# Linear attention feeding two expert layers: reciprocal denominators of query blocks 0 and 1 spread by TensorE, key tiles in units of 1024 columns

## Chip, cores, metric

The kernel runs on one core of a Trainium2 chip. The metric is the device time of one execution in microseconds (us). Engines are called as the profile calls them: PE (TensorE matmul), PEld (its weight load), DVE (VectorE), ACT (ScalarE), POOL (GpSimd), SP (SyncE, which issues the DMAs).

## What is computed

Attention with a feature map instead of a softmax, then a gated feed-forward, then a soft mixture of experts on the 2304 tokens. The change touches the attention alone:

```
def phi(x):
    proj = np.einsum('bhsd,df->bhsf', x, w_phi)
    proj = proj - np.max(np.abs(proj), axis=-1, keepdims=True)
    return np.concatenate([np.exp(proj), np.exp(-proj)], axis=-1)
q_p, k_p = (phi(q), phi(k))
kv = np.einsum('bhsf,bhsd->bhfd', k_p, v)
z = np.sum(k_p, axis=2)
num = np.einsum('bhsf,bhfd->bhsd', q_p, kv)
den = np.einsum('bhsf,bhf->bhs', q_p, z)[..., None] + 1e-06
return (num / den).astype(np.float32)
...
x = rms_norm(attention) ; silu(x @ w_gate) * (x @ w_val) @ w_out ; soft mixture of experts
```

There are 4 batches of 576 tokens, 8 heads of 64, and 128 features (256 with both signs).

## The kernel before, in words

**Key stage.** The 2304 tokens are 18 tiles of 128 keys. For each tile, `project` (L387) multiplies the keys of all 8 heads by `w_phi`, into two PSUM tiles of one bank each (`P`, half 0 the even heads and half 1 the odd ones, 4 x 128 columns each). DVE takes the largest absolute value of each head's row (`mx`, L398) and subtracts it (`pr`, L402), a pass for each half. ACT writes exp(pr) and exp(-pr) (`kp`, L415 and L416), again by halves: four calls of 512 columns. PE then adds the tile into `kacc`: `kv_of` (L439) values times features, four matmuls for each half, and `z_of` (L448) the sums of features with a column of ones, 32 output columns wide, four side by side. The loop at L519 issues the projection of tile i+1 ahead of the sums of tile i. A tile that crosses a batch border is summed in two parts, so there are 20 sums. At a border the sums are copied out (`Evac`, `kvs`) and turned (`kvt`).

**Weights.** The feed-forward's weights come as 64-bit numbers. Nine of 18 pieces are converted within the key stage, nine within the first block of the feed-forward: DMA into `wraw`, two ACT passes (L127, L129), two DVE passes (L137, L139), a cast on ACT and a subtraction on POOL (L102, L105).

**Queries.** They come in six blocks of 384 tokens. Blocks 0 and 1 are `Turned`: their projections, transposes (`T`) and exponentials (`e`, L339) are put between the key tiles (block 0) and into the feed-forward's block 0 (query block 1) by tables of slots, `TURNED0` and `TURNED1`; a slot is half a key tile or a third of a feed-forward step. Blocks 2 to 5 are `Reduced`. All use `attend` (L197): for each pair of heads PE computes `num` (numerators, 128 x 384) and `den` (denominators, in rows of 32 equal partitions: heads by halves of the block, 192 columns). ACT copies `num` to SBUF, DVE adds 1e-6 and takes the reciprocal (L218, L219). Eight ACT copies of 32 x 192 (L224) spread the reciprocals to 64 partitions for each head, and DVE multiplies (L225). A square and a sum for the RMS norm follow (L228 to L232), then in other slots `scale` and `out`.

**Feed-forward.** Six blocks of 384 tokens, each of 12 steps of gate (`pg`), value (`pv`) and output (`acc`) matmuls. Gate block 0 needs query block 0 complete; its own fillers make query block 1. The experts follow.

What decides the order on each engine: the Tile framework orders the instructions within what the program's issue order and data allow. Each engine runs its queue in order.

Of the kernel before, what the change touches and what calls it, by code (L numbers as in the profile page):

```python
# [64 lines left out]
def tile_kernel(ctx: ExitStack, tc: tile.TileContext, q2T, qT, kT, v, wbd, wg, wv, wo, rmsg, phi, w1, w2, consts, out):  # L65
# [120 lines left out]
    class Q:  # L186
# [10 lines left out]
        def attend(self, c):  # L197
# [22 lines left out]
            rd = e[1][:, 0].rearrange("p (g t) -> p g t", g=2)  # L220
            for hh, g in halves:
                o = 64 * hh + 32 * g
                for r in range(2):
                    ACT.copy(out=rd[64 * hh + 32 * r:64 * hh + 32 * r + 32, g], in_=dn[o:o + 32])  # L224
            DVE.tensor_tensor(out=y, in0=y, in1=e[1][:, 0], op=ALU.mult)  # L225
# [7 lines left out]
            for b, t0, t1 in block_parts(self.blk):  # L233
                if c == 3 and self.blk * BLK + t1 == (b + 1) * SEQ and b + 2 < NB:
                    kvt[b + 2] = kvp.tile([128, NH, 2, HD + 1], F32, tag="kv", name=f"kv{b + 2}", bufs=2)
                    SP.dma_start(out=kvt[b + 2].rearrange("p h s d -> p (h s d)"), in_=kv_d[b + 2])

# [18 lines left out]
    class Reduced(Q):  # L256
# [43 lines left out]
        def steps(self):  # L300
            def first():
                self.split(0)
                self.load(3)

            f = [lambda h=h: self.feature(h) for h in range(NH)]
            a = [lambda c=c: self.attend(c) for c in range(4)]
            g = [lambda h=h: self.exps(h) for h in range(NH)]
            s = [first, *(x for c in range(4) for x in (f[2 * c], f[2 * c + 1], g[2 * c], g[2 * c + 1], a[c])), self.scale, self.out]
            return sorted(zip(REDUCED, s), key=lambda x: x[0])

    class Turned(Q):
# [28 lines left out]

        def spare(self):
            e = self.sp.tile([128, 2, 2, BLK], F32, tag="e", name="dg", bufs=self.bufs["e"])
            return e[:, 0, 0], None
# [10 lines left out]
        def steps(self, at, attend, end, lag=2):  # L354


            r, pr = [], {}

            def p(c, i):
                pr[c, i] = self.project(c, i)  # L360

            for c in range(4):
                for i in range(TPB):
                    r.append((at[c] + i, lambda c=c, i=i: p(c, i)))
                    r.append((at[c] + i + lag, lambda c=c, i=i: self.turn(c, i, pr[c, i])))
                r.append((attend[c], lambda c=c: self.attend(c)))
            r += [(end[0], self.scale), (end[1], self.out)]
            return sorted(r, key=lambda x: x[0])

    with ExitStack() as pk:  # L370
# [5 lines left out]
        class Front:  # L376


            def __init__(self, sp, ps, src, i, bufs):
                self.sp, self.ps, self.src, self.i, self.bufs, self.tag = sp, ps, src, i, bufs, bufs["tag"]  # L380
                self.mx, self.pr, self.e = {}, {}, {}
# [5 lines left out]
            def project(self):  # L387

                tag, n = self.bufs["P"]
                self.p = [self.ps.tile([128, 4, DF], F32, tag=tag, name="P", bufs=n) for _ in range(2)]  # L390
                for c in range(4):
                    for hf in range(2):
                        r = slice(64 * hf, 64 * hf + 64)
                        PE.matmul(out=self.p[hf][:, c], lhsT=self.raw[r, c], rhs=wbd_f[r, DF * hf:DF * hf + DF], start=True, stop=True)  # L394

            def largest(self, hf):
                self.mx[hf] = mx = self.sp.tile([128, 4, 1], F32, tag=self.tag + "mx", name="mx", bufs=2)
                DVE.tensor_reduce(out=mx, in_=self.p[hf], axis=AX.X, op=ALU.max, apply_absolute_value=True)  # L398

            def less(self, hf):  # L400
                self.pr[hf] = pr = self.sp.tile([128, 4, DF], F32, tag=self.tag + "pr", name="pr", bufs=self.bufs["pr"])
                DVE.tensor_tensor(out=pr, in0=self.p[hf], in1=self.mx[hf].to_broadcast([128, 4, DF]), op=ALU.subtract)  # L402

            def shift(self, hf):
                self.largest(hf)
                self.less(hf)

        class K(Front):
# [4 lines left out]
            def exps(self, hf):  # L413
                kp = sp.tile([128, 4, 2, DF], F32, tag="kp", name="kp", bufs=4)
                ACT.activation(out=kp[:, :, 0], in_=self.pr[hf], func=AF.Exp)  # L415
                ACT.activation(out=kp[:, :, 1], in_=self.pr[hf], func=AF.Exp, scale=-1.0)  # L416
                self.e[hf] = kp
# [11 lines left out]
            def kv_of(self, hf, part):  # L429
                kp = self.e[hf]  # L430
# [12 lines left out]
            def z_of(self, hf, part):  # L443
                kp, za = self.e[hf], acc[part[0]][2]
# [46 lines left out]
        kb = {"tag": "k", "raw": 4, "pr": 3, "P": ("P", 2)}  # L491
        SP.dma_start(out=wbd_f, in_=wbd)
        ks = [K(sp, psk, kT, i, kb if i else dict(kb, P=("misc", 3))) for i in range(TILES)]
# [17 lines left out]
        for hf in range(2):  # L511
            ks[0].shift(hf)
            ks[0].exps(hf)
# [5 lines left out]
        for i in range(TILES):  # L519
# [18 lines left out]
            if kn:  # L538
                kn.project()
                kn.shift(0)  # L540
                kn.largest(1)
                conv_join()
                kn.less(1)
            k.kv(parts[-1])
            for hf in range(2):
                if kn:
                    kn.exps(hf)
# [513 lines left out]
```

## Time and profile before

| what | us |
|---|---|
| three timed runs | 751.07, 747.67, 746.72 (median 747.67) |
| the profiled execution | 745.82 |
| its span, first to last instruction | 743.8 |
| PE busy in the span | 714.6 (96%) |
| DVE busy | 428.1 (58%) |
| ACT busy | 371.2 (50%) |
| POOL busy | 108.3 (15%) |

A busy time is the union of an engine's instructions. Matmul ends are modelled, so a busy PE need not be a PE at its peak: matmuls on different rows or columns of the array can run side by side, and whether they do is seen from the start of one group to the start of the next. Matmuls in fp32 have two records each, so `x16` is eight matmuls. The program's stages follow each other: keys until about 133 us, the feed-forward until about 687, then the experts, where DMA is the busiest.

### The profile page before, as it was taken

To read this page: it belongs to the slowest core of one execution; us is meant where nothing else is said; L and a number is where in the kernel's file an instruction comes from. 1 tells how busy PE (TensorE), PEld (TensorE's weight loads), DVE (VectorE), ACT (ScalarE), POOL (GpSimd) and SP (SyncE) were. 2 spreads that over 40 slices of the span, in tenths; PEclk is the share of its full clock that TensorE was granted. 3 is DMA by queue.
4 is the path that set the end of the run, shared out by engine and by line. 5 is a ranking of instruction groups with operands and counts; after the bars stand their busy time and mean duration, and the time that the engine had idled before them with its cause. 6 is when DMAs were issued, how large, how long until landed. Compare 5 with 4: busy or idle time off the path is not lost.

```text
span 743.8 us, 12360 instructions
## 1 busy us (share of the span) xinstructions
PE 714.6 (96%) x4919; PEld 576.0 (77%) x4919; DVE 428.1 (58%) x808; ACT 371.2 (50%) x805; POOL 108.3 (15%) x60
## 2 busy tenths in 40 slices
PE   6999898999899999999999999999999999999994
PEld 4555554888789888898888988889888899988343
DVE  5888956688746557555575565655556453332413
ACT  6789854688644465344653446533465331212102
POOL 0222210134200112011120121101211010000100
PEclk9999999999999999999999999999999999999997
DMA  9674211545010100101000010000100046567898
GB/s 321 231 251 171 72 44 45 200 158 200 1 61 22 33 22 22 48 0 33 22 23 20 1 33 22 23 19 0 33 1 2 9 170 248 204 227 291 292 385 312
DMA packets 25145, 79.45 MB, mean 107 GB/s; under 512 B 2688, under 2 KB 13376, under 8 KB 18688
## 3 DMA queue, kind: packets, MB, share of 16 engines
q1 hardware_dynamic: 24864, 77.79, 29.6%
q10 hardware_dynamic: 224, 0.88, 0.4%
q8 instruction: 38, 0.62, 0.4%
q14 instruction: 19, 0.16, 0.1%
HBM read 71.99 MB, written 6.67 MB: 106 GB/s over the span
## 4 chain that ended last, share of the span: by engine, by line
PE 73%; ACT 10%; DVE 6%; DMA 5%; issue 2%; POOL 1%; SPq 0%; ACTq 0%; DVEq 0%; POOLq 0%
PE pv L794 18%; PE pg L794 17%; PE acc L819 6%; PE acc L820 6%; PE acc L821 6%; PE num L206 4%; PE kacc L439 3%; DMA eu<-in_w_dram 2%; PE den L214 2%; ACT e L224 2%; PE kacc L448 2%; DVE wt L137 1%; DMA wraw<-in_wg_dram 1%; ACT wt L127 1%; PE P L394 1%
## 5 line engine op out<-in xcount | busy, mean ns | idle before, releaser
L794 PE MATMUL pv<-xnh,wv 128*128 128x384 f32 x576 | 151.5, 344 | 0.0
L794 PE MATMUL pg<-xnh,wg 128*128 128x384 f32 x576 | 150.2, 342 | 1.2 <-DVE t L802 1.0
L794 PEld LDWEIGHTS pg<-xnh,wg 128*128 128x128 f32 x576 | 104.7, 188 | 7.2 <-DVE t L802 1.5
L794 PEld LDWEIGHTS pv<-xnh,wv 128*128 128x128 f32 x576 | 103.1, 188 | 7.0 <-issue 6.7
L794 PE MATMUL pv<-xnl,wv 128*128 128x384 f32 x288 | 97.7, 339 | 0.0
L794 PE MATMUL pg<-xnl,wg 128*128 128x384 f32 x288 | 97.5, 338 | 0.0
L819 PE MATMUL acc<-wo,hh 128*128 128x512 f32 x216 | 88.5, 410 | 0.4 <-ACT hh L102 0.4
L280 POOL PARTITION_ALL_REDUCE qe<-qe x32 | 50.0, 1561 | 262.7 <-ACT qe L279 243.0
L820 PE MATMUL acc<-wo,hh 128*128 128x512 f32 x216 | 85.8, 397 | 0.0
L821 PE MATMUL acc<-wo,hl 128*128 128x512 f32 x216 | 85.3, 395 | 0.0
L102 ACT CAST hh<-t 128x384 fp32r<-128x384 f32 x72 | 36.7, 510 | 80.9 <-PE acc L820 69.8
L105 DVE TENSOR_TENSOR hl<-t,hh 128x384 fp32r<-128x384 f32 x72 | 41.3, 574 | 53.7 <-ACT hh L102 51.2
L802 DVE SCALAR_TENSOR_TENSOR t<-t,pg 128x384 f32<-128x384 f32 x72 | 39.7, 551 | 51.7 <-ACT t L801 51.6
L801 ACT ACTIVATE t<-pg 128x384 f32<-128x384 f32 x72 | 35.1, 488 | 62.8 <-PE pg L794 62.8
L224 ACT COPY qe<-qe 32x192 f32<-32x192 f32 x128 | 44.8, 350 | 31.7 <-DVE qe L219 30.4
L806 DVE TENSOR_TENSOR t<-t,pv 128x384 f32<-128x384 f32 x72 | 39.7, 552 | 30.3 <-PE pv L794 29.0
L794 PEld LDWEIGHTS pg<-xnl,wg 128*128 128x128 f32 x288 | 54.0, 188 | 0.3 <-DVE xnl L105 0.3
L794 PEld LDWEIGHTS pv<-xnl,wv 128*128 128x128 f32 x288 | 54.1, 188 | 0.1
L439 PE MATMUL kacc<-kp,vt 128*64 128x256 f32 (+1 forms) x320 | 43.9, 399 | 5.4 <-ACT kp L416 5.3
L821 PEld LDWEIGHTS acc<-wo,hl 128*128 128x128 f32 x216 | 40.6, 188 | 9.8
L819 PEld LDWEIGHTS acc<-wo,hh 128*128 128x128 f32 x216 | 40.7, 189 | 8.1 <-ACT hh L102 0.9
L820 PEld LDWEIGHTS acc<-wo,hh 128*128 128x128 f32 x216 | 40.7, 188 | 6.5
(187 smaller groups left out, 1069.3 us busy)
## 6 DMA issues: line engine op xcount, KB each, us to landing
eu<-in_w_dram SPq DMA_DIRECT2D x32, 1024.0 KB, 6.0
wraw<-in_wg_dram SPq DMA_DIRECT2D x6, 1024.0 KB, 5.3
wraw<-in_wv_dram SPq DMA_DIRECT2D x6, 1024.0 KB, 6.5
wraw<-in_wo_dram SPq DMA_DIRECT2D x6, 1024.0 KB, 6.2
qraw<-in_qT_dram SPq DMA_DIRECT2D x32, 192.0 KB, 2.3
raw<-in_kT_dram SPq DMA_DIRECT2D x18, 256.0 KB, 3.7
vt<-in_v_dram SPq DMA_DIRECT2D x18, 256.0 KB, 2.9
out_dram<-ob SPq DMA_DIRECT2D x18, 256.0 KB, 3.4
```

The source lines that it names most:

```text
L102: ACT.copy(out=hi, in_=src)
L105: (lo_eng or POOL).tensor_tensor(out=lo, in0=src, in1=hi.bitcast(F32), op=ALU.subtract)
L224: ACT.copy(out=rd[64 * hh + 32 * r:64 * hh + 32 * r + 32, g], in_=dn[o:o + 32])
L280: POOL.partition_all_reduce(e[:, 0], e[:, 1], channels=128, reduce_op=bass_isa.ReduceOp.absmax)
L439: PE.matmul(out=kva[o0:o0 + 64, hh // 2], lhsT=self.vt[r0:r1, h], rhs=kp[r0:r1, hh].rearrange("p s f -> p (s f)"), start=first and hh < 2, ...
L794: PE.matmul(out=p, lhsT=w[:, a, c], rhs=x, start=n == 0, stop=n == 11)
L801: ACT.activation(out=t, in_=g, func=AF.Tanh, scale=0.5)
L802: DVE.scalar_tensor_tensor(out=t, in0=t, scalar=1.0, in1=g, op0=ALU.add, op1=ALU.mult)
L806: DVE.tensor_tensor(out=t, in0=t, in1=wide("v", m, xs), op=ALU.mult)
L819: PE.matmul(out=acc[i], lhsT=hh[:, s], rhs=w[:, 0], start=m == 0, stop=False)
L820: PE.matmul(out=acc[i], lhsT=hh[:, s], rhs=w[:, 1], start=False, stop=False)
L821: PE.matmul(out=acc[i], lhsT=hl[:, s], rhs=w[:, 0], start=False, stop=m == MF - 1)
```

## The change

Two things change.

*Spreading.* `attend` ends with the reciprocal. A new `normalise` does the multiply, the square and the rest. It takes the spread reciprocals from `wide`. In `Reduced` (query blocks 2 to 5) `wide` is the eight ACT copies as before, and `normalise` follows `attend` at once. In `Turned` (blocks 0 and 1) `wide` is four matmuls: a column of the identity matrix, repeated 64 times, picks the partition that holds a head's reciprocals and writes it to 64 partitions of a PSUM tile `rd`; and `normalise` stands one slot after `attend`. DVE then multiplies with `rd` from PSUM.

*Units.* A key tile's projection goes into one PSUM tile of two banks. `shift` is one maximum and one subtraction over 1024 columns, `exps` two calls over 1024 columns. The first tile keeps two PSUM tiles of one bank. The conversion pass that stood between the two halves' subtractions now follows the whole shift.

```
         dn = e[0][:, 0, 0:BLK // 2]
         DVE.tensor_scalar(out=dn, in0=den, scalar1=1e-6, scalar2=None, op0=ALU.add)
         DVE.reciprocal(out=dn, in_=dn)
-        rd = e[1][:, 0].rearrange("p (g t) -> p g t", g=2)
-        for hh, g in halves:
-            o = 64 * hh + 32 * g
-            for r in range(2):
-                ACT.copy(out=rd[64 * hh + 32 * r:64 * hh + 32 * r + 32, g], in_=dn[o:o + 32])
-        DVE.tensor_tensor(out=y, in0=y, in1=e[1][:, 0], op=ALU.mult)
+        self.left = e, dn
+
+    def normalise(self, c):
+        y = xraw[self.blk][:, c]
+        e, dn = self.left
+        DVE.tensor_tensor(out=y, in0=y, in1=self.wide(e, dn), op=ALU.mult)
...
+    def wide(self, e, dn):
+        rd = self.psum("rd", [128, BLK])
+        for g in range(2):
+            for hh in range(2):
+                o = 64 * hh + 32 * g
+                PE.matmul(out=rd[64 * hh:64 * hh + 64, BLK // 2 * g:BLK // 2 * g + BLK // 2], lhsT=ident[:, o:o + 1].to_broadcast([128, 64]),
+                          rhs=dn, start=True, stop=True, skip_group_check=True)
+        return rd
...
             r.append((attend[c], lambda c=c: self.attend(c)))
+            r.append((attend[c] + 1, lambda c=c: self.normalise(c)))
...
-            tag, n = self.bufs["P"]
-            self.p = [self.ps.tile([128, 4, DF], F32, tag=tag, name="P", bufs=n) for _ in range(2)]
+            tag, n, k = self.bufs["P"]
+            self.p = [self.ps.tile([128, k, DF], F32, tag=tag, name="P", bufs=n) for _ in range(8 // k)]
+            p = [self.p[0][:, 0:4], self.p[-1][:, k - 4:k]]
...
-        def shift(self, hf):
-            self.largest(hf)
-            self.less(hf)
+        def shift(self):
+            mx = self.sp.tile([128, 8, 1], F32, tag=self.tag + "mx", name="mx", bufs=2)
+            self.pr = self.sp.tile([128, 8, DF], F32, tag=self.tag + "pr", name="pr", bufs=self.bufs["pr"])
+            k = 8 // len(self.p)
+            for n, p in enumerate(self.p):
+                w = slice(k * n, k * n + k)
+                DVE.tensor_reduce(out=mx[:, w], in_=p, axis=AX.X, op=ALU.max, apply_absolute_value=True)
+                DVE.tensor_tensor(out=self.pr[:, w], in0=p, in1=mx[:, w].to_broadcast([128, k, DF]), op=ALU.subtract)
...
-            kp = sp.tile([128, 4, 2, DF], F32, tag="kp", name="kp", bufs=4)
-            ACT.activation(out=kp[:, :, 0], in_=self.pr[hf], func=AF.Exp)
-            ACT.activation(out=kp[:, :, 1], in_=self.pr[hf], func=AF.Exp, scale=-1.0)
+            self.e = kp = sp.tile([128, 2, 4, 2, DF], F32, tag="kp", name="kp", bufs=2)
+            kp = kp.rearrange("p h c s f -> p (h c) s f")
+            for s in range(2):
+                ACT.activation(out=kp[:, :, s], in_=self.pr, func=AF.Exp, scale=1.0 - 2.0 * s)
...
-    kb = {"tag": "k", "raw": 4, "pr": 3, "P": ("P", 2)}
+    kb = {"tag": "k", "raw": 4, "pr": 2, "P": ("P", 1, 8)}
...
             kn.project()
-            kn.shift(0)
-            kn.largest(1)
+            kn.shift()
             conv_join()
-            kn.less(1)
         k.kv(parts[-1])
+        if kn:
+            kn.exps()
```

How the instructions stand on the engines, at three places. The rows read: line, operation, out<-in, shape, how many.

PE in the key stage, before, around the projection of the fourth key tile (`P<-wbd_f,raw`; `P<-wbd_f,qraw` is a query's):

```order
L322 MATMUL P<-wbd_f,qraw 128x256 x2
L394 MATMUL P<-wbd_f,raw 128x128 x4
L439 MATMUL kacc_166<-kp,vt 64x256
L394 MATMUL P<-wbd_f,raw 128x128 x4
L439 MATMUL kacc_166<-kp,vt 64x256 x3
L448 MATMUL kacc_168<-kp,small 32x256
L439 MATMUL kacc_167<-kp,vt 64x256 x4
L448 MATMUL kacc_168<-kp,small 32x256 x7
```

The same place in the changed kernel:

```order
L332 MATMUL P<-wbd_f,qraw 128x256 x2
L414 MATMUL P<-wbd_f,raw 128x128 x8
L347 MATMUL T<-cst,qpr 128x128 x2
L457 MATMUL kacc_156<-kp,vt 64x256 x4
L457 MATMUL kacc_157<-kp,vt 64x256 x4
L466 MATMUL kacc_158<-kp,small 32x256 x8
```

The projection is whole, and one sum of z no longer stands alone between the two halves of kv. Of 18 projections three stood cut by halves with a sum between, and five z had one of their eight matmuls alone.

ACT around the first attend of query block 0, before (`wv`, `wo`, `wt`, `wraw` are the weight conversion):

```order
L102 CAST wo_1006<-wt 128x1024
L224 COPY e_298<-e_298 32x192 x8
L415 ACTIVATE kp<-pr 128x4x128
L416 ACTIVATE kp<-pr 128x4x128
L228 ACTIVATE s<-xraw 128x384
L415 ACTIVATE kp<-pr 128x4x128
L416 ACTIVATE kp<-pr 128x4x128
L216 COPY xraw<-num 128x384
```

And in the changed kernel, from the exponentials of the eighth key tile on:

```order
L435 ACTIVATE kp<-pr 128x8x128 x2
L216 COPY xraw<-num 128x384
L349 ACTIVATE e_482<-T 128x2x128 x2
L102 CAST wv_1177<-wt 128x1024
L127 ACTIVATE wt<-wraw 128x1024
L129 ACTIVATE wraw<-wraw 128x1024
L228 ACTIVATE s<-xraw 128x384
L435 ACTIVATE kp<-pr 128x8x128 x2
L216 COPY xraw<-num 128x384
L102 CAST wo_1244<-wt 128x1024
```

The copies are gone, and the conversion of all nine pieces ends with the cast of `wo_1244`, just after the exponentials of the ninth tile; before, the last cast (`wo_1397`) stood in the middle of the thirteenth's.

PE in the feed-forward's block 0, after the last denominators of the second attend of query block 1, before, from the last of nine output matmuls on:

```order
L821 MATMUL acc_1503<-wo_1397,hl 128x512
L322 MATMUL P<-wbd_f,qraw 128x256
L794 MATMUL pg<-xnh_1443,wg_1590 128x384 x2
L794 MATMUL pg<-xnl_1444,wg_1590 128x384
L794 MATMUL pg<-xnh_1447,wg_1590 128x384 x2
L794 MATMUL pg<-xnl_1448,wg_1590 128x384
L794 MATMUL pg<-xnh_1451,wg_1590 128x384 x2
```

And in the changed kernel:

```order
L836 MATMUL acc_1350<-wo_1244,hl 128x512
L809 MATMUL pg<-xnh_1290,wg_1437 128x384 x2
L809 MATMUL pg<-xnl_1291,wg_1437 128x384
L809 MATMUL pg<-xnh_1294,wg_1437 128x384 x2
L809 MATMUL pg<-xnl_1295,wg_1437 128x384
L356 MATMUL rd<-e_1630,cst 64x192 x4
L332 MATMUL P<-wbd_f,qraw 128x256
L809 MATMUL pg<-xnh_1298,wg_1437 128x384 x2
```

`rd` stands behind nine output and six gate matmuls after the denominators, and it reads the reciprocal that DVE makes from them.

## Rows read from the trace of the kernel before

**Rows 1.** Windows: from and to, length, busy us of PE, PEld, DVE, ACT, POOL, then PEclk, DMA

```profile
4.00:70.00 66.00, 62.16 (x578) 36.98 (x580) 52.18 (x79) 53.40 (x95) 14.71 (x6) 1.00 0.74 262
70.00:131.20 61.20, 56.07 (x537) 31.46 (x539) 43.99 (x81) 40.45 (x85) 7.55 (x3) 0.97 0.17 53
133.70:230.80 97.10, 93.97 (x570) 82.42 (x571) 72.00 (x115) 63.98 (x123) 23.03 (x9) 1.00 0.34 119
230.80:324.10 93.30, 93.01 (x563) 80.69 (x562) 54.19 (x108) 46.26 (x109) 15.01 (x9) 1.00 0.10 29
```

**Rows 2.** Groups on ACT, 0 to 132 us: count | busy us, mean ns | idle before

```profile
L224 ACT COPY e<-e 32x192 f32<-32x192 f32 x32 | 11.1, 348 | 2.4 <-DVE e L219 2.0
```

**Rows 3.** Groups on ACT, 133.7 to 230.8 us

```profile
L224 ACT COPY e<-e 32x192 f32<-32x192 f32 x32 | 11.2, 349 | 5.4 <-DVE e L219 5.1
```

**Rows 4.** Timeline of ACT, 54 to 66 us: start, duration, instruction, count, [idle before]

```profile
53.42 0.61 ACT L416 ACTIVATE kp<-pr 128x512 f32<-128x512 f32 x1
53.94 0.61 ACT L415 ACTIVATE kp<-pr 128x512 f32<-128x512 f32 x1
...
58.82 2.87 ACT L224 COPY e<-e 32x192 f32<-32x192 f32 x8
61.72 0.63 ACT L415 ACTIVATE kp<-pr 128x512 f32<-128x512 f32 x1
```

**Rows 5.** Timeline of DVE, 54 to 66 us

```profile
59.02 1.28 DVE L402 TENSOR_TENSOR pr<-P,mx 128x512 f32<-128x512 f32 x2
```

**Rows 6.** Timeline of PE, 52 to 66 us

```profile
51.85 1.07 PE L448 MATMUL kacc<-kp,small 128*32 128x256 f32 x16
52.85 1.51 PE L206 MATMUL num<-e,kv 128*64 128x384 f32 x8
...
63.23 0.67 PE L322 MATMUL P<-wbd_f,qraw 128*128 128x256 f32 x2 [0.88 <-DVE qpr L326]
```

**Rows 7.** Timeline of PE, 9 to 30 us

```profile
12.91 1.16 PE L394 MATMUL P<-wbd_f,raw 64*128 64x128 f32 x16
...
15.01 0.62 PE L448 MATMUL kacc<-kp,small 128*32 128x256 f32 x2
...
18.63 1.16 PE L394 MATMUL P<-wbd_f,raw 64*128 64x128 f32 x8
...
20.29 1.16 PE L394 MATMUL P<-wbd_f,raw 64*128 64x128 f32 x8
```

**Rows 8.** Timeline of DVE, 49 to 55 us

```profile
51.08 1.28 DVE L402 TENSOR_TENSOR pr<-P,mx 128x512 f32<-128x512 f32 x2
52.27 1.21 DVE L139 SCALAR_TENSOR_TENSOR wt<-wraw,wt 128x1024 uint32<-128x1024 uint32 x1
53.40 1.22 DVE L137 SCALAR_TENSOR_TENSOR wt<-wt,wraw 128x1024 uint32<-128x1024 uint32 x1
```

**Rows 9.** Timeline of ACT, 9 to 21 us

```profile
12.10 1.15 ACT L127 ACTIVATE wt<-wraw 128x1024 f32<-128x1024 f32 x1
13.16 1.13 ACT L129 ACTIVATE wraw<-wraw 128x1024 uint32<-128x1024 uint32 x1
```

**Rows 10.** Timeline of PE, 105 to 131.6 us

```profile
116.58 3.43 PE L439 MATMUL kacc<-kp,vt 128*64 128x256 f32 x16
...
123.21 1.95 PE L439 MATMUL kacc<-kp,vt 128*64 128x256 f32 x16
...
127.95 1.08 PE L439 MATMUL kacc<-kp,vt 128*64 128x256 f32 x8 [1.79 <-ACT kp L416]
```

**Rows 11.** Timeline of DVE, 171 to 189 us

```profile
181.23 1.35 DVE L219 RECIPROCAL e<-e 128x192 f32<-128x192 f32 x1
```

**Rows 12.** Timeline of PE, 174 to 184 us

```profile
180.10 0.52 PE L794 MATMUL pg<-xnh,wg 128*128 128x384 f32 x2
```

**Rows 13.** Waits of PE, 133 to 231 us: who <- whom, us in total, times, longest

```profile
PE pg L794 <- DVE t L802: 1.0, 1, 1.0
PE ssq L241 <- DVE s L232: 0.7, 1, 0.7
```

More of the change, by code (lines that the diff above doesn't have):

```diff
@@ L236, in attend @@
                     SP.dma_start(out=kvt[b + 2].rearrange("p h s d -> p (h s d)"), in_=kv_d[b + 2])
+        def wide(self, e, dn):
+            rd = e[1][:, 0].rearrange("p (g t) -> p g t", g=2)
+            for hh in range(2):
+                for g in range(2):
+                    o = 64 * hh + 32 * g
+                    for r in range(2):
+                        ACT.copy(out=rd[64 * hh + 32 * r:64 * hh + 32 * r + 32, g], in_=dn[o:o + 32])
+            return e[1][:, 0]
         def scale(self):
@@ L305, in steps @@
             f = [lambda h=h: self.feature(h) for h in range(NH)]
-            a = [lambda c=c: self.attend(c) for c in range(4)]
+            a = [lambda c=c: (self.attend(c), self.normalise(c)) for c in range(4)]
             g = [lambda h=h: self.exps(h) for h in range(NH)]
@@ L339, in turn, with wide @@
                 ACT.activation(out=self.e2[:, :, s, 128 * i:128 * i + 128], in_=tp, func=AF.Exp, scale=1.0 - 2.0 * s)
+        def wide(self, e, dn):
+            rd = self.psum("rd", [128, BLK])
+            for g in range(2):
+                for hh in range(2):
+                    o = 64 * hh + 32 * g
+                    PE.matmul(out=rd[64 * hh:64 * hh + 64, BLK // 2 * g:BLK // 2 * g + BLK // 2], lhsT=ident[:, o:o + 1].to_broadcast([128, 64]),
+                              rhs=dn, start=True, stop=True, skip_group_check=True)
+            return rd
         def spare(self):
@@ L380, in __init__ @@
                 self.sp, self.ps, self.src, self.i, self.bufs, self.tag = sp, ps, src, i, bufs, bufs["tag"]
-                self.mx, self.pr, self.e = {}, {}, {}
             def load(self):
@@ L393, in project @@
                         r = slice(64 * hf, 64 * hf + 64)
[L394 to L402, printed above, removed]
-            def shift(self, hf):
-                self.largest(hf)
-                self.less(hf)
+                        PE.matmul(out=p[hf][:, c], lhsT=self.raw[r, c], rhs=wbd_f[r, DF * hf:DF * hf + DF], start=True, stop=True)
+            def shift(self):
[6 more added lines that the diff above has]
+                    DVE.tensor_tensor(out=self.pr[:, w], in0=p, in1=mx[:, w].to_broadcast([128, k, DF]), op=ALU.subtract)
         class K(Front):
@@ L411, in load_v, with exps @@
                 SP.dma_start(out=self.vt, in_=v[self.i].rearrange("p (h d) -> p h d", h=NH))
-            def exps(self, hf):
-                kp = sp.tile([128, 4, 2, DF], F32, tag="kp", name="kp", bufs=4)
-                ACT.activation(out=kp[:, :, 0], in_=self.pr[hf], func=AF.Exp)
-                ACT.activation(out=kp[:, :, 1], in_=self.pr[hf], func=AF.Exp, scale=-1.0)
-                self.e[hf] = kp
+            def exps(self):
+                self.e = kp = sp.tile([128, 2, 4, 2, DF], F32, tag="kp", name="kp", bufs=2)
+                kp = kp.rearrange("p h c s f -> p (h c) s f")
+                for s in range(2):
+                    ACT.activation(out=kp[:, :, s], in_=self.pr, func=AF.Exp, scale=1.0 - 2.0 * s)
             def kv(self, part):
@@ L429, in kv_of @@
             def kv_of(self, hf, part):
-                kp = self.e[hf]
+                kp = self.e[:, hf]
                 b, r0, r1 = part
@@ L443, in z_of @@
             def z_of(self, hf, part):
-                kp, za = self.e[hf], acc[part[0]][2]
+                kp, za = self.e[:, hf], acc[part[0]][2]
                 first, last = self.ends(part)
@@ L489, in turn @@
                     SP.dma_start(out=kv_d[self.b], in_=kv.rearrange("p h s d -> p (h s d)"))
-        kb = {"tag": "k", "raw": 4, "pr": 3, "P": ("P", 2)}
+        kb = {"tag": "k", "raw": 4, "pr": 2, "P": ("P", 1, 8)}
         SP.dma_start(out=wbd_f, in_=wbd)
-        ks = [K(sp, psk, kT, i, kb if i else dict(kb, P=("misc", 3))) for i in range(TILES)]
+        ks = [K(sp, psk, kT, i, kb if i else dict(kb, P=("misc", 3, 4))) for i in range(TILES)]
         ks[0].load()
@@ L510, in tile_kernel @@
         ks[0].project()
-        for hf in range(2):
-            ks[0].shift(hf)
-            ks[0].exps(hf)
+        ks[0].shift()
+        ks[0].exps()
         fillers = []
@@ L539, in tile_kernel @@
                 kn.project()
-                kn.shift(0)
-                kn.largest(1)
+                kn.shift()
                 conv_join()
-                kn.less(1)
             k.kv(parts[-1])
+            if kn:
+                kn.exps()
             for hf in range(2):
-                if kn:
-                    kn.exps(hf)
                 if hf == 0 and i % 2:
```

## Prediction

> **What bounds the kernel now.** I read the windows first, then the timelines of TensorE (PE), ScalarE (ACT) and VectorE (DVE) around the edited lines, then the waits. The windows [rows 1], cut at the first gate matmul of each block, divide the work that the change touches into two stages. In the key stage, until 133.7 us, no engine is clearly the bound: in its first half (4 to 70) PE is busy 62 of 66 us, ACT 53 and DVE 52; in its second (70 to 131) PE 56 of 61, ACT 40, DVE 44. PE's share includes matmuls that run badly packed, as below. In gate block 0 (133.7 to 230.8) the matmuls of the feed-forward fill PE; the block takes 97.1 us, block 1 takes 93.3, and there ACT is busy 46 instead of 64. From block 1 on the program is the old one, so only these two stages can move.
>
> **The change, part by part.** All sums stand against the profiled execution, 745.82 us (span 743.8). The median of the three timed runs, 747.67, is 1.85 above it; I carry the difference over.
>
> *The copies.* Eight ACT copies per attend go: 32 x 0.348 us = 11.1 in the key stage [rows 2] and 11.2 in block 0 [rows 3]. What counts is who stands behind them. In the first attend they run from 58.82 to 61.7, and the next key exponential starts at 61.72 [rows 4], though DVE had the keys' second half ready at 59.02 + 1.28 = 60.3 and the first some 0.6 earlier [rows 5]: about 2.0 us late. DVE then sits in its multiply, and in the next attend PE waits 0.88 for a DVE result behind it [rows 6]. Four attends at 0.9 to 2.0 make 3.6 to 8.0; the low end for the sum is 0, should another engine be just as late. I take 1.1 each, -4.4, nearer to PE's own wait.
>
> *Whole units on PE.* Where the old order handled half 0 before half 1, PE lost its packing. A projection of 16 records takes 1.16 us, and so does one of 8 when the two halves are apart; a z of 2 records takes 0.62 [rows 7], when 16 take 1.07 [rows 6]. The order shows three projections cut that way (1.1 each) and five such z (0.4 each): 3.3 + 2.0 = 5.3. The new order has none. Two of the projections lie before 30 us, where ACT and DVE are as busy; so -3.0, between 0 and -5.3.
>
> *Issue.* One DVE pass over 1024 columns starts its successor 1.13 us later (52.27 to 53.40), two passes over 512 take 1.19 (51.08 to 52.27) [rows 8]: 0.06 x 2 passes x 17 tiles = 2.0 of DVE, of which I count 0.7. No row reads two PSUM banks in one instruction; the bounds are this 2.0 and 0, or a loss if the bank border cost something, which no row suggests. On ACT 512 columns start their successor 0.52 later (53.42 to 53.94) [rows 4], 1024 columns 1.06 later (12.10 to 13.16) [rows 9]: 2 x 0.52 against 1.06, nothing. I take the rows' starts, so 0 from ACT. [...]
>
> *The matmuls added.* rd is 4 matmuls of 192 columns, two column halves at a time; num, 4 of 384 in the same form, takes 1.51 [rows 6], so 0.75 per attend: +3.0 in each stage. In the key stage its cover would be PE's waits; I count it in full.
>
> *The first and last key tile* wait for two exponentials of 1.06 where 0.52 each was enough for half 0. The last kacc already waits 1.79 for ACT [rows 10]. I take +1.2 for both, from 0 to 2.
>
> *The clock.* At 116.6 one kacc run takes 3.43 us where the next takes 1.95 [rows 10], and the granted clock of that half is 0.97 [rows 1]: a stretch at 1.2 instead of 2.4 GHz, in which PE ran keys behind the fourth attend. It costs 1.5; I count half of it as gone, -0.7, from -1.5 to +1.5 (it may come elsewhere).
>
> Key stage: -4.4 - 3.0 - 0.7 + 3.0 + 1.2 - 0.7 = -4.6.
>
> *Block 0.* PE is the bound here, so rd costs its 3.0. It also stands in PE's queue and waits for DVE's reciprocal. At the second attend the reciprocal ended at 181.23 + 1.35 = 182.58 [rows 11]; in the new order rd stands in front of the seventh gate matmul, which started at 180.10 [rows 12]: a wait of 2.5 us, with everything on PE behind it. DVE was late because it waited in order for the weight conversion on ACT; eight copies fewer on ACT bring that forward, and PE arrives 0.75 later. The three other places can add up to 1. I take +1.5, from 0 to 3.5. In return PE's waits of 1.0 for t and 0.7 for s [rows 13], both behind the copies, go: -1.7. Block 0: 3.0 + 1.5 - 1.7 = +2.8, from +1.3 to +6.5.
>
> Sum: -4.6 + 2.8 = -1.8: 744.0 on the profiled execution's scale, **745.9 us** on the median's. What runs in ACT's place next is the exponentials waiting for DVE; what is late on PE next is rd.
>
> **The rivals.**
> - *PE's floor.* The copies cost their upper end and the splits all: -8.0 - 5.3 - 0.7 + 3.0 + 1.2 - 0.7 = -10.5, block 0 +2.8, together -7.7: 740.0. For it: after the ninth tile's exponentials there is one weight cast left in ACT's new order and no scaling, so PE can run through. Against it: the conversions that were there are now earlier, in the half where ACT and DVE are as full as PE. Chance 0.18.
> - *Cheaper activations.* ACT's durations, 0.348 for 192 columns [rows 2] and 0.61 for 512 [rows 4], make 0.82 ns a column and 0.19 us fixed. If the fixed part is time that ACT can't overlap in this mix of instructions, 36 key exponentials fewer give it 36 x 0.19 = 6.8 us, half of it on the path: 745.9 - 3.4 = 742.5. The start-to-start rows speak against it, and ACT's 53 of 66 us until 70 [rows 1] for it. [...] Chance 0.12.
> - *The unit is too long* (slower). From a projection's end a tile needs two DVE passes of 1.13 and two exponentials of 1.06, 4.4 us, before its first kacc; before, half of that unit was enough: three passes of 0.6 and two of 0.52, 2.8. PE has kacc, z and the next projection to cover it, 1.95 + 1.07 + 1.16 [rows 10, 6, 7], near 4.0 without their tails. Where no query work lies between, PE waits 0.4, and with one conversion pass of 1.1 ahead in DVE's or ACT's queue 1.5. It decides where the 4.4 plus what is queued exceeds PE's own work. At 0.6 a tile over 17 tiles, +10.2: -4.6 + 10.2 + 2.8 = +8.4, 756.1. For it: the conversion fills ACT and DVE until 70. Against it: until now tiles come every 6 to 7 us (18 in 127), above 4.4. Chance 0.10.
> - *rd blocks PE.* All four waits of block 0 stay and nothing comes back: 3.0 + 3.5 = 6.5, sum +1.9: 749.6. Chance 0.12.
>
> **How the numbers follow.** 0.5% of 747.67 is 3.7 us, about what a measurement can tell from no change. My forecast has 0.48, spread over 743 to 749, since its terms are sums of halves. Faster by over 0.5% (under 743.9): the floor, most of the cheaper activations, a little of the forecast: 0.32. Slower (over 751.4): the long unit, and the edge of the blocked PE: 0.13. The rest, 0.55, is no change that can be told. The range 739.5 to 751 takes in the floor and the blocked PE, and leaves out most of the long unit and the outermost of each.
>
> **What would show it.** Right: the first gate matmul starts near 129 (133.7 before), no 2-record z, exponentials of 1024 columns start their successor after about 1.05; block 0 lasts near 100 with PE waiting for DVE's reciprocal in front of rd. Wrong: kacc waiting for ACT in most tiles (the long unit); a gate start near 124 (the floor); block 0 at 97 (rd hidden after all) or over 103.

## The result, and the profile after

| | median us (runs) | lowest to highest |
|---|---|---|
| before | 748.06 (4) | 746.72 to 751.07 |
| after | 757.37 (4) | 756.59 to 759.54 |

The ratio is 1.013 [1.0109, 1.0151]: slower by 9.7 us of 748 (8.2 to 11.3). I had predicted 745.9, with 739.5 to 751 as the range. The profiled execution after is 759.54 us long (span 757.8), the slowest of the four, while the one before, 745.82, is among the fastest of its kernel. So stages of the profiles tell *where* the time went, and the ratios *how much*. (The quotients of the medians shown beside the ratios differ from them by up to 0.2%, or 1.4 us.)

Windows of the changed kernel, cut as in [rows 1] (from and to, length, busy us of PE, PEld, DVE, ACT, POOL, then PEclk, DMA share, GB/s):

```profile
4.00:70.00 66.00, 56.34 (x504) 33.26 (x506) 52.72 (x56) 49.46 (x62) 20.72 (x8) 0.92 0.72 252
70.00:137.80 67.80, 63.04 (x642) 36.67 (x642) 43.12 (x70) 30.60 (x50) 2.36 (x1) 0.98 0.18 57
140.50:243.20 102.70, 98.64 (x602) 85.91 (x603) 76.71 (x116) 53.63 (x92) 23.62 (x9) 0.98 0.32 113
243.20:336.50 93.30, 93.01 (x563) 80.76 (x562) 53.41 (x107) 45.84 (x108) 15.01 (x9) 1.00 0.10 29
```

The first gate matmul starts at 140.5 instead of 133.7, gate block 0 takes 102.7 instead of 97.1, and block 1 its old 93.3. The loss lies in the two stages that the change touches. ACT is some 10 us less busy than in [rows 1] from 70 on, and 10 in block 0, and both stages are longer all the same. Until 70 PE is busy 56 us where it was 62, and its granted clock is 0.92.

**Key stage.** Waits of PE from 0 to the first gate matmul (who <- whom, us in total, times, longest), first before, then after:

```profile
PE kacc L439 <- ACT kp L416: 5.3, 6, 1.8
```

```profile
PE kacc L457 <- ACT kp L435: 10.9, 8, 2.9
```

Three of the eight waits are long. Timeline of PE after (start, duration, instruction, count, idle before it and its releaser):

```profile
10.58 3.68 PE L457 MATMUL kacc<-kp,vt 128*64 128x256 f32 x16 [2.87 <-ACT kp L435]
...
54.00 1.95 PE L457 MATMUL kacc<-kp,vt 128*64 128x256 f32 x16 [0.58 <-ACT kp L435]
...
63.33 2.82 PE L457 MATMUL kacc<-kp,vt 128*64 128x256 f32 x10 [2.69 <-ACT kp L435]
...
133.85 2.75 PE L457 MATMUL kacc<-kp,vt 128*64 128x256 f32 x16 [2.83 <-ACT kp L435]
```

After 0.58 of waiting the 16 records of a sum take their 1.95 us. After 2.69 ten records take 2.82, and after 2.83 sixteen take 2.75: these waits are paid a second time, in the clock behind them. The first sum takes 3.68 because PE still runs at 1.2 GHz, but that isn't shown to come from its wait: e9 and e7 (below) wait 1.42 there and are as slow. And the longest low stretch after the start has another occasion: in the six us before it PE waits only 0.83 (at 34.64) and 0.35. Its window, with PEclk as the third number from the end:

```profile
39.30:46.10 6.80, 6.80 (x36) 3.68 (x32) 3.86 (x6) 4.62 (x8) 1.12 (x2) 0.50 0.88 327
```

What the tile at 63.3 waited for stands in ACT's timeline, and in DVE's:

```profile
59.28 1.16 ACT L127 ACTIVATE wt<-wraw 128x1024 f32<-128x1024 f32 x1 [2.48 <-POOL wo L105]
60.33 1.04 ACT L102 CAST wg<-wt 128x1024 fp32r<-128x1024 f32 x1
61.27 2.01 ACT L435 ACTIVATE kp<-pr 128x1024 f32<-128x1024 f32 x2
```

```profile
56.94 1.22 DVE L423 TENSOR_TENSOR pr<-P,mx 128x1024 f32<-128x1024 f32 x1
```

The subtracted projections were there at 58.16. ACT's queue had a conversion pass (which waited 2.48 us for POOL) and a cast ahead of the exponentials, and then the first sum needs both whole exponentials, 2.01 us.

**Block 0.** Waits of PE after, 140.5 to 243.2, and the one of before in its block 0 that [rows 13] don't have:

```profile
PE rd L356 <- DVE e L219: 4.0, 2, 3.3
```

```profile
PE num L206 <- ACT e L339: 1.2, 1, 1.2
```

The old waits (1.2 here, 1.0 and 0.7 in [rows 13]) are all gone from the list, and one line has taken their place. Timelines after around its longest wait, DVE, then POOL, then PE:

```profile
186.68 0.35 DVE L218 TENSOR_SCALAR e<-den 128x192 f32<-128x192 f32 x1
186.95 3.13 DVE L139 SCALAR_TENSOR_TENSOR wt<-wraw,wt 128x1024 uint32<-128x1024 uint32 x1
190.00 1.34 DVE L219 RECIPROCAL e<-e 128x192 f32<-128x192 f32 x1
```

```profile
186.32 2.66 POOL L105 TENSOR_TENSOR wo<-wt,wo 128x1024 fp32r<-128x1024 f32 x1 [4.31 <-ACT wo L102]
```

```profile
187.50 0.51 PE L809 MATMUL pg<-xnh,wg 128*128 128x384 f32 x2
187.86 0.34 PE L809 MATMUL pg<-xnl,wg 128*128 128x384 f32 x1
191.48 0.87 PE L356 MATMUL rd<-e,cst 128*64 128x192 f32 x8 [3.29 <-DVE e L219]
192.28 0.70 PE L332 MATMUL P<-wbd_f,qraw 128*128 128x256 f32 x2
192.63 0.98 PE L809 MATMUL pg<-xnh,wg 128*128 128x384 f32 x2
```

The reciprocal directly follows the addition of 1e-6 in the program; in DVE's queue a pass of the weight conversion stands between them. In the kernel before it stood there too, and took 1.22:

```profile
179.83 0.35 DVE L218 TENSOR_SCALAR e<-den 128x192 f32<-128x192 f32 x1
180.10 1.22 DVE L139 SCALAR_TENSOR_TENSOR wt<-wraw,wt 128x1024 uint32<-128x1024 uint32 x1
```

Beside a POOL pass it takes 3.13 us. `rd` waits 3.29 for it, with all gate matmuls queued behind, and two of these then take 0.98 instead of 0.51: 1.2 GHz again.

The block's accounts close: PE is busy 98.64 against 93.97 [rows 1], +4.7, of which four `rd` runs at 0.80 from start to start are 3.2 and the half clock the rest; idle grew by 0.9 (4.06 against 3.13), the new wait less the old ones.

### The profile page after: what moved, and what is told of

It is laid out like the page before. It is cut to its first block, busy times and chain, and to the rows that moved or that the text cites. A ratio compares the mean times of both kernels' runs of the same rounds, so it can differ in the third digit from the quotient of the medians.

```text
span 757.8 us, 12324 instructions
## 1 busy us (share of the span) xinstructions
PE 721.6 (95%) x4983; PEld 580.9 (77%) x4983; DVE 431.5 (57%) x774; ACT 346.5 (46%) x705; POOL 109.7 (14%) x60
## 4 chain that ended last, share of the span: by engine, by line
PE 81%; DVE 6%; DMA 5%; ACT 5%; issue 1%; SPq 1%; POOL 0%; ACTq 0%; DVEq 0%
PE pv L809 19%; PE pg L809 18%; PE acc L834 6%; PE acc L835 6%; PE acc L836 6%; PE num L206 4%; PE kacc L457 3%; DMA eu<-in_w_dram 2%; DMA wraw<-in_wg_dram 2%; PE den L214 2%; PE kacc L466 2%; PE y L948 2%; DVE wt L137 2%; DVE wt L139 1%; ACT kp L435 1%
## 5 line engine op out<-in xcount | busy, mean ns | idle before, releaser
L105 DVE TENSOR_TENSOR hl<-t,hh 128x384 fp32r<-128x384 f32 x72 | 46.0, 638 | 58.3 <-ACT hh L102 55.9
L457 PE MATMUL kacc<-kp,vt 128*64 128x256 f32 (+1 forms) x320 | 44.4, 417 | 11.3 <-ACT kp L435 10.9
L435 ACT ACTIVATE kp<-pr 128x1024 f32<-128x1024 f32 x36 | 36.3, 1055 | 23.8 <-DVE pr L423 23.8
L834 PEld LDWEIGHTS acc<-wo,hh 128*128 128x128 f32 x216 | 40.8, 189 | 8.1 <-ACT hh L102 0.9
```

The lines of the kernel that those rows point to most:

```text
L105: (lo_eng or POOL).tensor_tensor(out=lo, in0=src, in1=hi.bitcast(F32), op=ALU.subtract)
L435: ACT.activation(out=kp[:, :, s], in_=self.pr, func=AF.Exp, scale=1.0 - 2.0 * s)
L457: PE.matmul(out=kva[o0:o0 + 64, hh // 2], lhsT=self.vt[r0:r1, h], rhs=kp[r0:r1, hh].rearrange("p s f -> p (s f)"), start=first and hh < 2, ...
L834: PE.matmul(out=acc[i], lhsT=hh[:, s], rhs=w[:, 0], start=m == 0, stop=False)
```

## The experiments

For e1 to e4 theory A said that the long unit holds TensorE back, B that the spreading and its slot cost in both stages, C that the new order of the weight conversion is the loss. The later expectations say in brackets what each letter then stands for. The code under each heading shows the lines that matter, not the whole edit.

| run | median us (runs) | ratio to before | us of 748 |
|---|---|---|---|
| the change | 757.37 (4) | 1.013 [1.0109, 1.0151] | +9.7 |
| e1 spreading alone | 751.55 (6) | 1.0051 [1.003, 1.0073] | +3.8 |
| e2 unit alone | 750.78 (10) | 1.0046 [1.0016, 1.0075] | +3.4 |
| e3 change, exponentials by halves | 753.14 (4) | 1.007 [1.0051, 1.009] | +5.2 |
| e4 spreading, block 1 two slots later | 751.08 (5) | 1.0062 [1.0039, 1.0086] | +4.6 |
| e5 e3, copies in query block 1 | 747.20 (12) | 1.0007 [0.998, 1.0034] | +0.5 |
| e6 e3, block 1 two slots later | 750.25 (12) | 1.003 [1.0016, 1.0044] | +2.2 |
| e7 unit, exponentials by halves, no spreading | 747.40 (12) | 0.9997 [0.9978, 1.0016] | -0.2 |
| e8 copies one slot later, nothing else | 747.84 (12) | 0.9997 [0.9982, 1.0013] | -0.2 |
| e9 change, first tile by halves | 757.25 (5) | 1.0144 [1.0118, 1.0171] | +10.8 |
| e10 change, short calls, signs outside | 758.75 (5) | 1.0149 [1.012, 1.0178] | +11.1 |
| e11 spreading in query block 1 alone | 753.60 (6) | 1.0084 [1.006, 1.0109] | +6.3 |
| e12 e5 with the copies one slot later | 746.54 (12) | 0.9997 [0.9976, 1.0018] | -0.2 |

### The two parts, each alone

```
# e1: the kernel before with the spreading's edits only
+ DVE.tensor_tensor(out=y, in0=y, in1=self.wide(e, dn), op=ALU.mult)
+ r.append((attend[c] + 1, lambda c=c: self.normalise(c)))
# e2: the kernel before with the unit's edits only
+ kb = {"tag": "k", "raw": 4, "pr": 2, "P": ("P", 1, 8)}
+ ACT.activation(out=kp[:, :, s], in_=self.pr, func=AF.Exp, scale=1.0 - 2.0 * s)
```

> The kernel before with the spreading alone: blocks 0 and 1 spread their reciprocals with four PE matmuls one slot later, key tiles stay in halves. Theory A (the unit lengthens the chain from a projection to the first sum, PE waits and its clock falls): the key stage loses nothing, the first gate matmul starts at 130 to 134 us (133.7 before, 140.6 in the changed kernel), at most one stretch of low clock in it; block 0 still takes 100 to 103 (97.1 before), total +1 to +6 over before. Theory B (rd and the slot are the loss everywhere): first gate matmul at 137 or later, total +8 to +12. Theory C (only the new order of the weight conversion, which needs both edits, is the loss): first gate matmul at 130 or earlier and no new low clock.

> The kernel before with the units of 1024 columns alone; the eight ACT copies stay. Theory A: first gate matmul at 138 to 142 us, PE waits for ACT's kp of 8 us or more in all (5.3 before), two or more low-clock stretches in the key stage; block 0 as before, 97 to 98; total +5 to +9. Theory B: first gate matmul within 1 of 133.7, total within 1 of before. Theory C: between 133 and 136, total +1 to +3.

Each part loses by itself, 3.8 and 3.4 us. Their sum, 7.2, is less than 9.7, but the intervals reach from 2.2 to 5.5, 1.2 to 5.6 and 8.2 to 11.3, so an interaction isn't shown. e1's total is theory A's, but its first gate matmul came at 135.9, later than A's 130 to 134. e2's total lies under A's +5 to +9 and just over C's +1 to +3, and its first gate matmul (137.3) between the two; only its waits for kp (10.4 us at nine sums) are as A had them. What e2 shows best is a pair of windows: PE's work in the key stage, before (to its first gate matmul) and in e2 (to its own):

```profile
0.00:133.70 133.70, 120.52 (x1130) 70.00 (x1130) 97.83 (x165) 97.65 (x188) 22.47 (x13) 0.99 0.46 158
```

```profile
0.00:137.30 137.30, 113.84 (x1131) 67.84 (x1131) 98.97 (x132) 94.71 (x152) 23.10 (x13) 0.96 0.46 153
```

PE is busy 6.7 us less, at a lower clock, and the stage is 3.6 us longer. The whole units did give PE its packing back; PE is idle 23.5 us instead of 13.2.

### The exponential: its length, its order, its first tile

```
# e3: the changed kernel, four calls in the place of two
+ for h in (slice(0, 4), slice(4, 8)):
+     for s in range(2):
+         ACT.activation(out=kp[:, h, s], in_=self.pr[:, h], func=AF.Exp, scale=1.0 - 2.0 * s)
# e10: the same four calls, loops exchanged
+ for s in range(2):
+     for h in (slice(0, 4), slice(4, 8)):
# e9: e3's halves for the first tile only
+ for h in (slice(0, 4), slice(4, 8)) if self.i == 0 else (slice(0, 8),):
```

> The changed kernel with the key exponentials called by halves again (four ACT calls of 512 columns a tile); projection and shift stay units of 1024. Theory A: the first sum of a tile no longer waits for the second half's 1.06 us; PE's waits for kp fall from 10.9 to 5 to 8 us, first gate matmul at 136 to 139 (140.6 in the changed kernel), total 2 to 4 under the changed kernel. Theories B and C: no change beyond 1 us.

> The changed kernel with the first tile of keys alone exponentiated by 512 columns; the other nine tiles keep 1024. Theory A1 (the key stage's loss is at the start: the first key sum waits 2.9 us instead of 1.5 and the clock comes late): most of the 4.2 us come back, 753 to 754 us. Theory A2 (the loss is a longer wait of TensorE at most tiles): a tenth to a quarter comes back, 756 to 757 us. Rival C (the conversion's order): no change from 757.4.

> The changed kernel with exponentials of 512 columns, but both halves with the plus sign first and then both with the minus sign, so that the first half is complete only behind the third of four calls. Theory A (what costs is how long TensorE waits for the first half): between halves and wholes, nearer to wholes, 755 to 757 us. Rival (a 1024-column instruction is itself the loss, by holding ScalarE or by its store): 753.1 us as with halves in order (752 to 754).

e3 gives 4.5 us back (9.7 to 5.2, where A had 2 to 4), and e7 against e2 says the same of the unit alone (-0.2 to 3.4). The edit leaves the place of the calls in the program as it was, but not the order on the engines: the framework makes that anew. Counted in ACT's traces, so many key tiles have their exponentials ahead of each of the nine weight casts:

| run | tiles ahead of the first to the ninth cast | us of 748 |
|---|---|---|
| before | 2.5, 4.5, 5, 6.5, 8, 8, 11, 11.5, 12.5 | 0 |
| the change | 2, 3, 4, 5, 6, 7, 7, 8, 9 | +9.7 |
| e2 | 2, 3, 4, 5, 6, 7, 7, 8, 10 | +3.4 |
| e9 | 3, 3, 5, 6, 6, 7, 8, 8, 10 | +10.8 |
| e10 | 3, 3, 5, 5, 6, 7, 8, 8, 10 | +11.1 |
| e3 (e5, e6, e12 likewise) | 3, 4, 5, 6, 7, 8, 8, 9, 10 | +5.2 |
| e7 | 3, 4, 5, 6, 7, 8, 8, 11, 11 | -0.2 |

With calls by halves the conversion comes about a tile later, in both pairs. So C isn't ruled out: e2 shows that the early conversion needs the units alone, not both edits, and no run changes the calls and keeps the order. e9 and e10, with casts in between and the whole loss, fit C badly.

ACT's own time isn't it: two calls of 1024 take less than four of 512. Timeline of ACT, after, then e3:

```profile
8.52 2.00 ACT L435 ACTIVATE kp<-pr 128x1024 f32<-128x1024 f32 x2 [5.05 <-DVE pr L423]
```

```profile
46.12 2.17 ACT L436 ACTIVATE kp<-pr 128x512 f32<-128x512 f32 x4
```

But of the four the first half is complete after two. e10 keeps the short calls and makes the first half wait for three (in all but the first tile, where the framework put the halves in order again). The trace shows it: calls start 0.52 apart and the third ends at 63.89, just before the sum. ACT, then PE, in e10:

```profile
62.22 2.19 ACT L436 ACTIVATE kp<-pr 128x512 f32<-128x512 f32 x4
```

```profile
63.95 1.97 PE L458 MATMUL kacc<-kp,vt 128*64 128x256 f32 x13 [2.62 <-ACT kp L436]
```

All of the gain is gone (+11.1). So the 1024 columns in one instruction are not the loss by themselves; what the slow runs share is a later first half, and an order of the queues that isn't e3's. That the wait for the first half is the cause is the likelier reading, but it isn't shown alone. I had expected e10 between the two; it came out at the slow end, though its first half is only 0.5 us later than e3's and the change's 0.9 (in e3, e10 and the change the sum starts 1.2, 1.7 and 2.1 us behind the first call's start). The loss is not in proportion to that. Waits of PE in the key stage, e3, e10, e9, and last e7:

```profile
PE kacc L458 <- ACT kp L436: 4.9, 6, 2.2
```

```profile
PE kacc L458 <- ACT kp L436: 9.8, 6, 2.7
```

```profile
PE kacc L458 <- ACT kp L436: 7.7, 8, 2.8
```

```profile
PE kacc L438 <- ACT kp L416: 7.5, 6, 2.6
```

These sums don't give the price: e7's is as long as e9's, and e7 loses nothing by its runs. One profile of this stage is a rough measure. e3, e5 and e6, whose edits leave the key stage the same, reach the first gate matmul at 133.8, 138.0 and 137.6 us.

e9 tests whether the start alone is to blame, where the wait of 2.87 and the late clock are easiest to see. It isn't: with the first wait back at 1.42 the time stays (+10.8), and 7.7 us of waits remain. So the other 17 tiles (the "nine" of the expectation is a slip) bear the loss, A2. How much of it the last one bears, whose wait stays at 2.83 in e9, no run tells. (In e9's profile the clock still comes late, the first 8 records of a sum taking 1.97 us; so it clears the wait at the start, not the clock there. But e7's clock comes as late, and e7 loses nothing.) PE in e9, its first sum and a later one, then the first sum of e7:

```profile
9.58 1.97 PE L458 MATMUL kacc<-kp,vt 128*64 128x256 f32 x8 [1.42 <-ACT kp L436]
...
52.81 3.68 PE L458 MATMUL kacc<-kp,vt 128*64 128x256 f32 x16 [0.85 <-ACT kp L436]
```

```profile
9.95 1.98 PE L438 MATMUL kacc<-kp,vt 128*64 128x256 f32 x8 [1.42 <-ACT kp L416]
```

### Block 0: wait, matmuls, slot

```
# e4 (on e1) and e6 (on e3): query block 1 normalised two slots later
+ r.append((attend[c] + (1, 2)[self.blk], lambda c=c: self.normalise(c)))
# e11 (on before): only query block 1 spread by PE; block 0 copies at once
+ r.append((attend[c] + (self.blk == 1), lambda c=c: self.normalise(c)))
# e5 (on e3): query block 1 copies at once, block 0 spread by PE
+ r.append((attend[c] + (self.blk == 0), lambda c=c: self.normalise(c)))
# e8 (on before): copies, but in the later slot, both blocks
+ r.append((attend[c] + 1, lambda c=c: self.normalise(c)))
```

> As the spreading alone, but in query block 1 (feed-forward block 0) normalise stands two slots after attend. If rd's 4.0 us of waiting for the reciprocal and the low clock behind it are what block 0 lost beyond rd's own 3.0: block 0 takes 98 to 100 instead of 100 to 103, PE's wait of rd for DVE under 1, no low clock; the total 2 to 5 under the spreading alone. If rd's own time and the misc PSUM buffer are the loss: no change, or worse by a wait of a projection or transpose for a buffer.

> The changed kernel with two edits: each tile's exponentials are four instructions of 512 columns (half by half, in the same place), and query block 1 (the one worked in expert block 0) spreads its reciprocals by ScalarE's copies in the slot of the attention, as the kernel before does; query block 0 keeps the spreading by TensorE one slot later. Theory A (two causes that add: the 1024-column exponential holds back the first key sum of each tile, and in block 0 TensorE stops at the spreading): with four 512-column calls the time was 753.1 us, and block 0's 5.2 us come back, so 747.9 us (746.5 to 749.5), block 0 97.0 us long. Theory B (the spreading costs 3 us of TensorE wherever it stands): 753.1 less only block 0's 5.2 plus nothing, with the key stage 2 to 3 us late, so 749.5 to 750.5. Theory C (the pair of parts interacts in the order of the weight conversion): 751 to 753.

> The changed kernel with exponentials of 512 columns and query block 1 normalised two slots after the attention. Theory A: block 0 keeps the 3.0 us of the spreading's matmuls and loses the wait for the reciprocal and what the clock takes behind it (block 0 102.2 to 100.3 us), so 753.1 - 1.9 = 751.2 us (750 to 752.5). Rival (the wait costs nothing, since TensorE makes it up at the block's end): 752.6 to 753.5.

> The kernel before with the normalising moved one slot behind the attention in query blocks 0 and 1, and the spreading left to ScalarE's copies: the slot without TensorE. Theory A (TensorE's spreading and its wait are the loss): no loss, 746.5 to 748.5 us, block 0 96 to 97.5 us long. Rival (the later slot itself costs, since the scale and the residual start later): 749.5 to 751.5, block 0 99 us or longer.

> The kernel before with the spreading by TensorE one slot later in query block 1 alone (expert block 0); the key stage as before. Theory A (block 0 alone bears the spreading's loss and the key stage is neutral): 748.0 + 5.2 = 753.2 us, or 751.5 if the whole loss of the spreading in both blocks (3.8 us) is block 0's. Rival (the key stage's spreading costs 2 us as its profile read): 749.5 to 750.

e11 has the key stage as before (first gate matmul at 133.7 in both) and loses 6.3, no less than e1 with both blocks (+3.8; the intervals meet). So the price of the spreading lies in block 0, which takes 102.1 us, much as in the change.

```profile
133.70:235.80 102.10, 98.64 (x601) 85.82 (x602) 76.65 (x116) 53.75 (x91) 23.59 (x9) 0.98 0.32 113
```

e8 clears the slot: a later `normalise` with ACT's copies costs nothing that can be measured (-0.2, from -1.3 to 1.0). e5 takes the spreading out of block 0 and gets nearly all of e3's rest back (5.2 to 0.5). That rests on its twelve runs, which go from 744.0 to 755.1; its profile is of the longest, and there block 0 takes 99.7 us and not the 97.0 that I expected, with one wait of 2.57 of PE for ACT before `num` and 1.2 GHz behind it. Two slots later instead of one (e6) gets 3.0 of it back. Window, wait of PE and timeline of DVE in e6's block 0:

```profile
137.60:238.00 100.40, 97.81 (x602) 84.10 (x603) 74.79 (x115) 52.69 (x91) 22.67 (x9) 1.00 0.33 115
```

```profile
PE rd L356 <- DVE e L219: 1.0, 1, 1.0
```

```profile
185.66 0.34 DVE L218 TENSOR_SCALAR e<-den 128x192 f32<-128x192 f32 x1
185.93 1.21 DVE L139 SCALAR_TENSOR_TENSOR wt<-wraw,wt 128x1024 uint32<-128x1024 uint32 x1
187.06 1.34 DVE L219 RECIPROCAL e<-e 128x192 f32<-128x192 f32 x1
```

The conversion pass still stands ahead of the reciprocal, now without POOL beside it; 1.0 of the wait is left, and the clock is 1.00 throughout. What remains against 97.1 is mostly the matmuls. e4, the same edit on e1, should have come 1.9 us below e1 by the blocks' lengths (I had expected 2 to 5); by the ratios it came 0.8 above, by the medians 0.5 below, within both intervals, so e4 alone decides nothing. How the 5 to 6 us divide between the matmuls and the wait is known only roughly: 1.7 and 3.0 by the ratios of e3, e6 and e5; 3.2 for the matmuls by their rows.

### What is left without the costs

```
# e7: before + the unit, with e3's loops in exps
# e12: e5, and the copies of query block 1 one slot later
+ r.append((attend[c] + 1, lambda c=c: self.normalise(c)))
```

> The kernel before with the unit of 1024 columns alone (one PSUM tile of two banks, one maximum and one subtraction of 1024 columns), but exponentials of 512 columns; no part of the spreading. Theory A (of the unit only the exponential's length costs): 747.7 us (746.5 to 749), no difference that can be measured, with the first gate matmul at 131 to 134 us in the profile. Rival (the two-bank unit itself costs, since TensorE fills one tile while VectorE holds the other): 750.5 to 751.5 as with the whole unit alone.

> A version put together from what held: unit of 1024 columns for projection, maximum and subtraction, exponentials of 512 columns, spreading by TensorE in query block 0 alone, and in query block 1 ScalarE's copies one slot behind the attention. Theory A: no loss is left and little gained, 746.5 us (745 to 748). Rival (copies behind the slot hold ScalarE's weight conversion in block 0): 748.5 to 750.

e7 keeps the unit for the projection, maximum and subtraction: no difference (-1.6 to 1.2). Its profile, of a run of 750.21 us, doesn't show that: the first gate matmul stands at 138.8, where I had expected 131 to 134. e12 puts together what cost nothing: no difference from before (0.9976 to 1.0018), though ACT in the key stage and PE's cut projections are relieved. No version that beats the kernel before was found.

```profile
135.50:232.00 96.50, 93.95 (x569) 82.50 (x570) 70.68 (x112) 62.82 (x120) 23.16 (x9) 1.00 0.34 120
```

Its block 0 is the shortest of all, 0.6 below [rows 1], and it doesn't show in the median.

## Why the prediction was wrong

The key stage was forecast at -4.6 and came out near +5 (9.7 less the 4.7 between e3 and e5); block 0 was forecast at +2.8 and came out at 4.7 by these runs, 5.6 by its length in the profiles.

*Whole units on PE (-3.0) and issue (-0.7).* This step failed first. The work that I counted did go: e2's PE is busy 6.7 us less. But I had read that no engine is the bound in the key stage, and then still sold PE's work at half its price. Nothing came of it: e7, with whole projections and shifts (and three sums of z with a 2-record part, where before had five), is at -0.2 (-1.6 to 1.2). Where a chain over several engines sets the pace, here, as the waits suggest, from projection over DVE and ACT to the first sum, work taken off PE becomes a wait, as in e2's 23.5 us of idle time.

*First and last tile (+1.2).* The mechanism was seen and counted at two tiles of 18. PE waits at eight sums, 10.9 us in all against 5.3, and behind two of the three long waits it runs at 1.2 GHz. Measured: 4.5 us, e3 against the change, with what the other order of the queues has in it. I had taken the unit of 1024 columns for free on ACT since its calls do not add up to more (2.00 against 2.17, even a little less), and had not asked when its first half ends, nor what order the framework would make of the longer calls.

*The rival "the unit is too long"* comes nearest to what happened in this stage, and I gave it 0.10. Its point of decision, 4.4 us and what is queued ahead against PE's own 4.0, is what the tile at 63.3 shows, with a conversion pass and a cast ahead in ACT's queue. I argued against it with tiles that come every 6 to 7 us. That is a mean, and says nothing of the single chain: PE fills the spacing with query work and sums, which stand in its queue *around* the key sum and cover the wait only where they stand ahead of it. Its 756.1 is near the result, but partly by luck: it charged 10.2 us to the unit, where 4.5 were measured, and 2.8 to block 0, where it was 4.7 to 5.6.

*The copies (-4.4) and rd (+3.0) in the key stage.* A net gain of 1.4 was forecast. e5 against e7 (which differ by this alone) says 0.7 slower, e1 against e11 2.5 faster; both intervals hold zero or nearly so. A gain isn't shown. In e1's profile PE's wait of 0.88 behind the multiply [rows 6] is gone, and one of 1.5 for ACT has come ahead of a transpose at 74.7.

*The clock (-0.7 in the key stage, none in block 0).* The sign was wrong in both. I asked whether the old stretch at half clock would go, not what the new waits would do to the clock. The profile after has a granted clock of 0.92 until 70 and 0.98 in block 0, where [rows 1] have 1.00 and 1.00. Not all of that stands behind the new waits (39.3 to 46.1 doesn't).

*Block 0 (+2.8, from 1.3 to 6.5).* The bounds held; the value was too low. `rd` cost its 3.0 (3.2 by its rows). The waits that I expected back came back, and the one for `num` with them (2.9). The wait for the reciprocal was put at the second attend, in front of the seventh gate matmul, at 2.5 us, and there it is, with 3.29. But I took 1.5, because eight copies fewer on ACT would bring DVE forward. DVE did come forward: the addition started 1.5 us before `rd`'s turn (186.68 against 188.20), and before it had started 0.3 before the seventh gate matmul (179.83 against 180.10). What I hadn't counted is the conversion pass between L218 and L219: beside POOL it takes 3.13 instead of 1.22, and these 1.9 us are more than was won. With 4.0 for the wait and the half clock behind it the block comes to the 5.6 measured.

*Cheaper activations.* The rows after do show a saving, 0.17 us per tile, or about 3 us of ACT over 18 tiles; it doesn't show in the time. The rival's 0.19 us a call is the fixed part of a lone duration, and calls in a row overlap: 0.61 long, they start 0.52 apart [rows 4], so that a call fewer saves 0.09. The Trainium skill (ScalarE: Activation LUTs, "What ACT_TABLE_LOAD costs") has both, 186 ns and 0.833 ns a column for an ACTIVATE with immediate operands, and an overlap of about 93 ns between back-to-back ones. An estimate from these figures is 0.19 us for two calls fewer; the trace's 0.17 agrees.

## What to carry over

Merging two halves into one instruction makes the work smaller and the first result later. Where an engine waits for that first result, count the time from the input to the *first* consumer, with what stands ahead in each queue, and not the sum of the instructions; e3 and e10 have the same four calls, and their order, with what the framework makes of it, is worth 6 us.

Where a framework orders the instructions, an edit of one call can reorder every queue. Before saying that two runs differ in one thing, compare the orders in their traces; here the weight conversion moved by a tile with the length of the exponentials.

A small operation that moves onto the engine that is the bound (four matmuls, 0.8 us) brings its input's whole delay along, since everything behind it in that queue waits too. Before moving it, look in the producer's queue for what stands between the two instructions that the program writes next to each other.

## What was not expected of the hardware

A DVE pass over 1024 columns that takes 1.21 us alone took 3.13 beside a POOL subtraction of 1024 columns (2.66). It began while the subtraction ran and ended 1.1 us behind its end (190.08 against 188.98). In the changed kernel's profile eight of the thirteen conversion passes that began while a POOL subtraction ran took 1.89 to 3.13 us and ended 1.1 behind it; the other five don't fit this. It isn't new with the change: the kernel before has one of 3.28 (at 32.42).

PE's granted clock was at its 1.2 GHz level right behind single waits of 2.7 to 3.3 us within otherwise busy stretches: behind 3.29 us a pair of gate matmuls took 0.98 instead of 0.51, while behind waits of 0.6 (54.00 above) and of 1.0 (e6) it stayed at 2.4 GHz. Not every such wait did it. In e7 the last sum waits 2.65 and runs at full clock behind it:

```profile
133.01 1.08 PE L438 MATMUL kacc<-kp,vt 128*64 128x256 f32 x8 [2.65 <-ACT kp L416]
```

Long waits aren't its only occasion either: in the changed kernel the clock was low from 39.3 to 46.1, and in e9 the sum at 52.81 ran at that level (3.68 us) behind a wait of 0.85, with 1.89 us of idle time before a projection at 49.81. No rule comes out of these runs. Block 0 shows what it adds there: 3.29 us of wait, and some 1.5 of busy time on top.
